# First 256 tokens' output products on f16 halves split by GpSimd, and the weights' own products read from the magnitude tiles

## The chip, the cores and the metric

One core of one Trainium2 chip runs the whole program. The metric is the device time of one launch in microseconds (us); the kernel before takes 868.63 us, the median of three runs.

## The reference

Causal attention with a decay bias, then a feed-forward stage. All inputs come as 64-bit floats, cut here to what is computed:

```python
B, H, S, D = 8, 8, 576, 64                        # q, k, v: [B, H, S, D], s: [B, H, S]
scores = q @ k.transpose(0, 1, 3, 2) / sqrt(D)
cum = cumsum(maximum(s, 0), axis=-1)
bias = -(cum[:, :, :, None] - cum[:, :, None, :])
scores = where(causal, -1e9, scores + minimum(bias, 0))
attn = softmax(scores)
x = (attn @ v).transpose(0, 2, 1, 3).reshape(4608, 512)
h = maximum(maximum(x @ w1, x @ w2), x @ w3)       # w1, w2, w3: [512, 768]
out = h @ w_out                                   # w_out: [768, 512]
```

## The kernel before, in words

**Steps.** The attention is cut into 160 steps. A step is one block of 128 queries (the last of a batch has 64) of one pair of heads. Batches 0 and 1 are visited first with their query blocks 0 and 1, all four pairs of heads, then with their blocks 2, 3, 4; batches 2 to 7 follow whole. In step t the program issues, in this order: work entered with `soon` for this step, a first number of feed-forward groups, the scores of step t+2, work entered with `amid`, the softmax of step t, work entered with `at` (`todo`), a second number of groups, and the products with v. [...]

**Softmax chain.** TensorE (PE) writes the scores `s`, VectorE (DVE) takes their maximum `nm`, ScalarE (ACT) the exponential and its sum `se`, DVE the reciprocal `ri`, ACT the f16 high halves `prh`, DVE the f16 low halves `prl`; DMAs transpose them and PE multiplies with v into `av`. The scores of a later step wait for `prl` of an earlier one, since they reuse its accumulation banks.

**Feed-forward groups.** When all heads of a set of 256 or 320 tokens are done, groups of matmuls for the set are put into `queue`. GROUPS gives for each step how many leave the queue before the scores and how many after. The first set (tokens 0 to 255 of batch 0, `PLAIN`, `add_plain`) is computed in 32-bit floats: 18 groups `up` (4 matmuls of 256 columns each) and 4 groups `down` (6 matmuls each). Every 32-bit matmul leaves two records in the trace. All other sets use f16 high and low halves of both factors: 18 groups `h_group` of 12 matmuls and 4 groups `o_group` of 18. The groups of `up` are maximised in `hs`, two tiles of 128x768 f32; `down` reads them.

**Weights.** The 24 weight tiles arrive as 64-bit words in `r` (`raw_w`) and are decoded by a chain: `decode1` (ACT) makes the 32-bit magnitude tile `t` (`half`, 3 buffers), `shift`, `low_bits` and `sign` (DVE, lines 872, 876, 883) complete it, and `sign` writes the finished f32 weight back over the low words. Later `decode3` (ACT) and `decode4` (DVE, L939) make the f16 halves `w`. A common power of two for the f16 scale comes from `gram1` (L894): the weights' bf16 top halves multiplied with themselves, summed in a corner of the bank `av`; its maximum goes through `wscale1` and `wscale2`. Tiles 0 to 17 (kind "u") give one scale, 18 to 23 ("d") the other. `gram1` reads the raw 64-bit words, so successive values lie 8 bytes apart. It is issued in parts of 5, 4, 4, 2, 3 tiles and of 4, 2: the last part of each kind ahead of the scores (`soon`), the others after them (`at`).

```python
top = raw_w[i].bitcast(BF16).rearrange("p (n t) -> p n t", t=4)[:, :, 1]
for c in range(NKT):
    blk_c = top[:, c * P:(c + 1) * P]
    nc.tensor.matmul(gr, lhsT=blk_c, rhs=blk_c, ...)
```

GpSimd (POOL) has little to do in the first 120 us; from batch 1's first f16 set on it casts and subtracts the f16 halves of the hidden values (L972, L973), and it makes a part of the keys' low halves `qkl` (L494).

Of the kernel before, what the change touches and what calls it, by code (L numbers as in the profile page):

```python
# [21 lines left out]
def kernel(  # L22
# [828 lines left out]


    PLAIN = {(0, 0)}
    W = {}
    fresh = {}
    T = {}
# [7 lines left out]
        return w[:, :, 0], w[:, :, 1]  # L864

    def decode1(i):
        half[i] = moe.tile([P, N], F32, tag="t", name=f"t{i}", bufs=3)
        nc.scalar.activation(out=half[i], in_=words(i)[1], func=AF.Copy, scale=2.0 ** -112)

    def shift(i):  # L870
# [8 lines left out]

    def sign(i):  # L880
        lo, hi = (x.bitcast(I32) for x in words(i))
        ti = half.pop(i).bitcast(I32)
        nc.vector.scalar_tensor_tensor(
            out=lo, in0=hi, scalar=-(2 ** 31), in1=ti, op0=ALU.bitwise_and, op1=ALU.bitwise_or
        )
        new[i] = words(i)[0].rearrange("p (a c) -> p a c", c=P)

    def gram1(kind, n, ids, of):
        gr = bank[:, 3 * P:4 * P]
        for a, i in enumerate(ids):  # L890
# [61 lines left out]
    def add_set(b, ph):  # L952
        q0, nq = PH[ph]
        t0 = b * S + q0
        u = f"{b}_{ph}"
        xs = [(t[:, 0], t[:, 1]) for t in X.pop((b, ph))]
        st = {}

        def h_group(ft, i):
            pm = ps_m.tile([P, 512], F32, tag="m", name=f"pm{u}_{ft}_{i}")  # L960
            w = W[3 * ft + i]
            n = 0
            for kt in range(NKT):
                xh, xl = xs[kt]
                for wt, xt in ((0, xh), (0, xl), (1, xh)):
                    nc.tensor.matmul(  # L966
                        pm[:, :nq], lhsT=w[:, wt, kt, :], rhs=xt, start=(n == 0), stop=(n == 3 * NKT - 1)
                    )
                    n += 1

            def rest(m1):
                nc.gpsimd.tensor_copy(out=st["hh"][:, ft, :nq], in_=m1[:, :nq])  # L972
                nc.gpsimd.tensor_tensor(  # L973
                    out=st["hl"][:, ft, :nq], in0=m1[:, :nq], in1=st["hh"][:, ft, :nq], op=ALU.subtract
                )

            def ev():
                if i == 0:
                    st["m1"] = moe.tile([P, 320], F32, tag="m1", name=f"m1{u}_{ft}", bufs=3)
                    nc.scalar.activation(out=st["m1"][:, :nq], in_=pm[:, :nq], func=AF.Copy, scale=HSC)  # L980
                else:
                    m1 = st["m1"]
                    nc.vector.scalar_tensor_tensor(  # L983
                        out=m1[:, :nq], in0=pm[:, :nq], scalar=HSC, in1=m1[:, :nq], op0=ALU.mult, op1=ALU.max
                    )
                if i == 2:
                    if not st.get("hh"):
                        st["hh"] = moe.tile([P, NFT, 320], F16, tag="hh", name=f"hh{u}")
                        st["hl"] = moe.tile([P, NFT, 320], F16, tag="hlo", name=f"hl{u}")
                    later.append(lambda m1=st["m1"]: rest(m1))  # L990

            pending.append(ev)
            if (ft, i) == (NFT - 1, 2):
                done.add((b, ph))

        def o_group(dt):
            drain()
            flush()
            if dt == 0:
                st["os"] = small.tile([P, 1], F32, tag="os", name=f"os{u}")  # L1000
                nc.gpsimd.tensor_scalar(
                    out=st["os"], in0=OS[b, ph if b < NB else 1], scalar1=WS["kw"], scalar2=None, op0=ALU.mult
                )
            pm = ps_m.tile([P, 512], F32, tag="m", name=f"po{u}_{dt}")
            n = 0
            for ft in range(NFT):
                for wt, ht in ((0, "hh"), (0, "hl"), (1, "hh")):
                    nc.tensor.matmul(  # L1008
                        pm[:, :nq], lhsT=W[18 + ft][:, wt, dt, :], rhs=st[ht][:, ft, :nq],
                        start=(n == 0), stop=(n == 3 * NFT - 1),  # L1010
                    )
# [12 lines left out]
        for dt in range(NDT):
            queue.append((lambda dt=dt: o_group(dt), W, range(18, 24), 18 * nq * NSEC))

    def add_plain(b, ph):
        q0, nq = PH[ph]
        t0 = b * S + q0
        u = f"{b}_{ph}"  # L1030
        xs = X.pop((b, ph))
        hs = {}

        def up(ft, i):
            pm = ps_m.tile([P, 512], F32, tag="m", name=f"pm{u}_{ft}_{i}")
            for kt in range(NKT):
                nc.tensor.matmul(
                    pm[:, :nq], lhsT=T[3 * ft + i][:, kt, :], rhs=xs[kt], start=(kt == 0), stop=(kt == NKT - 1)
                )

            def ev():
                a = ft // 3
                if a not in hs:
                    hs[a] = moe.tile([P, 3, nq], F32, tag=("hh", "hlo")[a], name=f"h{u}_{a}")
                m1 = hs[a][:, ft % 3]
                if i == 0:
                    nc.scalar.activation(out=m1, in_=pm[:, :nq], func=AF.Copy)
                else:
                    nc.vector.tensor_tensor(out=m1, in0=pm[:, :nq], in1=m1, op=ALU.max)

            pending.append(ev)
            if (ft, i) == (NFT - 1, 2):
                done.add((b, ph))

        def down(dt):
            drain()
            pm = ps_m.tile([P, 512], F32, tag="m", name=f"po{u}_{dt}")
            for ft in range(NFT):
                nc.tensor.matmul(
                    pm[:, :nq], lhsT=T[18 + ft][:, dt, :], rhs=hs[ft // 3][:, ft % 3], start=(ft == 0), stop=(ft == NFT - 1)  # L1060
                )

            def ev():
                o_t = moe.tile([P, 320], F32, tag="m1", name=f"o{u}_{dt}", bufs=3)
                nc.scalar.activation(out=o_t[:, :nq], in_=pm[:, :nq], func=AF.Copy)
                nc.sync.dma_start(out=outT[dt * P:(dt + 1) * P, t0:t0 + nq], in_=o_t[:, :nq])

            pending.append(ev)

        for ft in range(NFT):  # L1070
            for i in range(3):
                queue.append((lambda ft=ft, i=i: up(ft, i), T, (3 * ft + i,), 16 * nq * NSEC))
        for dt in range(NDT):
            queue.append((lambda dt=dt: down(dt), T, range(18, 24), 24 * nq * NSEC))

    later = []

# [36 lines left out]
    def soon(t, f, *a):  # L1114
        early.setdefault(t, []).append((f, a))
# [51 lines left out]
    def at(t, f, *a):  # L1167
# [28 lines left out]
    )  # L1196
    GROUPS = (
# [13 lines left out]
    )  # L1211
    scaled = {}
    for kind, tiles, parts in (("u", range(18), (5, 4, 4, 2, 3)), ("d", range(18, 24), (4, 2))):
        ids = sorted(tiles, key=lambda i: begun[i])
        scaled[kind] = end = begun[ids[-1]] + 2
        for n, size in enumerate(parts):
            part = ids[sum(parts[:n]):sum(parts[:n + 1])]
            t = begun[part[-1]] + 2
            (soon if t == end else at)(t, gram1, kind, n, part, len(parts))
        at(end, wscale1, kind)  # L1220
    at(scaled["d"] + 1, wscale2, "d")
    for v in range(NP, len(visits), NP):
# [211 lines left out]
```

## Time and profile before

| | |
|---|---|
| three runs | 867.27, 868.63, 869.16 us |
| span of the profiled execution | 867.7 us; the page gives no other time for it, so its own time is taken as 867.7, 0.9 us under the median |
| PE busy | 815.8 us, 94% |
| DVE busy | 629.2 us, 73% |
| ACT busy | 542.7 us, 63% |
| POOL busy | 287.2 us, 33% |
| chain that ended last | PE 51%, of it the first feed-forward products (L966) 31% |

The table is read from the page of the profiled execution. Shares are averages over a program whose stages differ: an opening in which weights are decoded, a long middle in which attention and feed-forward groups alternate on PE, and a tail of some 88 us without attention. Times inside the program are counted from the start of the span.

### The profile page before, as it was taken

To read this page: it belongs to the slowest core of one execution; us is meant where nothing else is said; L and a number is where in the kernel's file an instruction comes from. 1 tells how busy PE (TensorE), PEld (TensorE's weight loads), DVE (VectorE), ACT (ScalarE), POOL (GpSimd) and SP (SyncE) were. 2 spreads that over 40 slices of the span, in tenths; PEclk is the share of its full clock that TensorE was granted. 3 is DMA by queue.
4 is the path that set the end of the run, shared out by engine and by line. 5 is a ranking of instruction groups with operands and counts; after the bars stand their busy time and mean duration, and the time that the engine had idled before them with its cause. 6 is when DMAs were issued, how large, how long until landed. Compare 5 with 4: busy or idle time off the path is not lost.

```text
span 867.7 us, 19554 instructions
## 1 busy us (share of the span) xinstructions
PE 815.8 (94%) x6929; PEld 617.7 (71%) x6929; DVE 629.2 (73%) x1562; ACT 542.7 (63%) x1458; POOL 287.2 (33%) x532
## 2 busy tenths in 40 slices
PE   5888998989998989899999999999999999999998
PEld 3777777766675667666777677776776678767875
DVE  6979977767778778787887869786878777662110
ACT  5878785576576666656776667666676676653111
POOL 1001115734423324345242524352334425211211
PEclk9999999999999989999999999999999999999999
DMA  9933577866777667765776767767876556433000
GB/s 353 357 89 82 123 160 151 189 151 122 153 153 146 126 156 169 156 120 141 146 167 140 144 135 145 153 129 155 175 154 127 117 111 125 103 75 70 13 14 31
DMA packets 238466, 119.84 MB, mean 138 GB/s; under 512 B 210592, under 2 KB 219296, under 8 KB 238368
## 3 DMA queue, kind: packets, MB, share of 16 engines
q1 hardware_dynamic: 237792, 117.01, 60.4%
q10 hardware_dynamic: 576, 1.57, 0.5%
q8 instruction: 55, 0.90, 0.4%
q14 instruction: 43, 0.35, 0.2%
HBM read 45.12 MB, written 9.44 MB: 63 GB/s over the span
## 4 chain that ended last, share of the span: by engine, by line
PE 51%; DVE 5%; ACT 2%; issue 2%; DMA 1%; SPq 0%; DVEq 0%; ACTq 0%
PE pm L966 31%; PE po L1008 10%; PE av L834 4%; PE s L541 4%; DVE prl L706 2%; PE s L552 1%; ACT prh L703 1%; DVE fixed L161 1%; DVE s L644 1%; DVE m L983 1%; DMA fixed<-in_pair_dram 0%; ACT s L663 0%; DMA pl<-prl 0%; ACT fixed L157 0%; DVE vl L520 0%
## 5 line engine op out<-in xcount | busy, mean ns | idle before, releaser
L966 PE MATMUL pm<-x,w 128*128 128x320 f16 (+1 forms) x3240 | 425.2, 288 | 0.0
L966 PEld LDWEIGHTS <-w 128*128 128x128 f16 x3240 | 312.3, 98 | 90.7 <-issue 4.1
L703 ACT ACTIVATE prh<-s,ri 128x512 f16<-128x512 f32 (+3 forms) x272 | 136.6, 548 | 125.6 <-DVE ri L687 124.4
L706 DVE SCALAR_TENSOR_TENSOR prl<-s,ri,prh 128x512 f16<-128x512 f32 (+3 forms) x272 | 147.0, 577 | 54.6 <-ACT prh L703 31.0
L972 POOL CAST hh<-m 128x320 f16<-128x320 f32 (+1 forms) x90 | 46.2, 513 | 353.8 <-DVE m L983 264.8
L663 ACT ACTIVATE s<-s,nm 128x128 f32<-128x128 f32 (+4 forms) x272 | 145.0, 533 | 17.1 <-DVE nm L644 11.5
L983 DVE SCALAR_TENSOR_TENSOR m<-pm,m 128x320 f32<-128x320 f32 (+1 forms) x180 | 82.1, 456 | 98.1 <-PE pm L966 78.4
L1008 PE MATMUL po<-hh,w 128*128 128x320 f16 (+1 forms) x720 | 142.0, 288 | 0.0
L1008 PEld LDWEIGHTS <-w 128*128 128x128 f16 x1080 | 104.1, 98 | 29.9 <-issue 1.4
L644 DVE CUSTOM_DVE_ANT_0 s<-s,later,qf 128x128 f32<-128x128 f32 (+1 forms) x192 | 106.1, 552 | 14.8 <-PE s L541 11.0
L1008 PE MATMUL po<-hl,w 128*128 128x320 f16 (+1 forms) x360 | 103.6, 288 | 0.0
L186 POOL COPY h<-fixed 64x576 f16<-64x576 f16 x96 | 68.1, 736 | 57.3 <-DVE fixed L161 55.9
L980 ACT ACTIVATE m<-pm 128x320 f32<-128x320 f32 (+1 forms) x90 | 36.6, 407 | 71.9 <-PE pm L966 70.6
L973 POOL TENSOR_TENSOR hl<-m,hh 128x320 f16<-128x320 f32 (+1 forms) x90 | 70.2, 780 | 7.4
L1016 ACT ACTIVATE o<-po,os 128x320 f32<-128x320 f32 (+1 forms) x60 | 30.0, 500 | 55.9 <-PE po L1008 52.1
L834 PEld LDWEIGHTS <-vh 128*64 128x64 f16 x800 | 43.9, 111 | 22.7 <-issue 16.3
L541 PE MATMUL s<-h 128*128 128x128 f16 (+1 forms) x192 | 42.2, 299 | 12.6 <-DVE prl L706 10.8
L663 ACT ACTIVATION_READ_ACCUMULATOR s<-s,nm 128x1 f32 x272 | 53.9, 198 | 0.0
L834 PE MATMUL av<-ph,vh 128*64 128x320 f16 (+3 forms) x368 | 48.8, 286 | 1.7 <-DMA ph<-prh 1.7
L834 PE MATMUL av<-ph,vl 128*64 128x320 f16 (+3 forms) x368 | 44.2, 278 | 0.0
L161 DVE SCALAR_TENSOR_TENSOR fixed<-fixed,qf,fixed 128x576 f16<-128x576 f32 x48 | 42.7, 924 | 1.0 <-ACT fixed L157 0.9
L541 PE MATMUL s<-l 128*128 128x128 f16 (+1 forms) x192 | 41.9, 299 | 0.0
(204 smaller groups left out, 1055.4 us busy)
## 6 DMA issues: line engine op xcount, KB each, us to landing
fixed<-in_pair_dram SPq DMA_DIRECT2D x24, 576.0 KB, 4.5
r<-in_w_dram SPq DMA_DIRECT2D x22, 512.0 KB, 8.3
rv<-in_qkv_dram SPq DMA_DIRECT2D x32, 320.0 KB, 3.5
h<-fixed SPq DMA_DIRECT2D x48, 144.0 KB, 3.4
l<-fixed SPq DMA_DIRECT2D x48, 144.0 KB, 3.6
out_dram<-o SPq DMA_DIRECT2D x32, 160.0 KB, 2.0
out_dram<-o SPq DMA_DIRECT2D x32, 128.0 KB, 1.9
raw<-in_qkv_dram SPq DMA_DIRECT2D x8, 480.0 KB, 3.7
```

Of the source, the lines that this page charges most:

```text
L161: nc.vector.scalar_tensor_tensor(out=u[:, 3 - 3 * x], in0=R[v][("rq", "rk")[x]], scalar=QK[visits[v][0]]["qk"[x]], in1=u[:, 1 + x], op0=AL ...
L186: nc.gpsimd.tensor_copy(out=R[v]["h"][own, j, x], in_=staged(v)[own, 3 - x])
L541: nc.tensor.matmul(ps[:, j, :nk], lhsT=w[:, c, qs], rhs=w[:, 1 - c, 0:nk], start=(x == "h"), stop=(x == "l"), skip_group_check=True,)
L644: nc.vector.tensor_tensor_reduce(out=sc[:, j], in0=sc[:, j], in1=future[0][:, Q4 - nk:Q4], scale=n, scalar=3.0e38, op0=ALU.add, op1=ALU.mi ...
L663: nc.scalar.activation(out=E[t][:, j, :nk] if plain else sc, in_=sc, func=AF.Exp, bias=nm[:, j:j + 1], scale=-1.0 if below(t) else 1.0, ac ...
L703: nc.scalar.activation(out=hi, in_=src, func=AF.Copy, scale=sc)
L706: nc.vector.scalar_tensor_tensor(out=lo, in0=src, scalar=sc, in1=hi, op0=ALU.mult, op1=ALU.subtract)
L834: nc.tensor.matmul(av[j * D:(j + 1) * D, c0:nq], lhsT=lt, rhs=rt, start=(n < 2), stop=(n >= len(todo) - 2), skip_group_check=True,)
L966: nc.tensor.matmul(pm[:, :nq], lhsT=w[:, wt, kt, :], rhs=xt, start=(n == 0), stop=(n == 3 * NKT - 1))
L973: nc.gpsimd.tensor_tensor(out=st["hl"][:, ft, :nq], in0=m1[:, :nq], in1=st["hh"][:, ft, :nq], op=ALU.subtract)
L983: nc.vector.scalar_tensor_tensor(out=m1[:, :nq], in0=pm[:, :nq], scalar=HSC, in1=m1[:, :nq], op0=ALU.mult, op1=ALU.max)
L1008: nc.tensor.matmul(pm[:, :nq], lhsT=W[18 + ft][:, wt, dt, :], rhs=st[ht][:, ft, :nq], start=(n == 0), stop=(n == 3 * NFT - 1),)
```

## The change

1. `gram1` takes one tile, reads the top halves of the magnitude tile `t` (values 4 bytes apart), and all tiles are issued with `soon`, two steps after their `decode1`, ahead of the scores. The tiles `t` get 5 buffers, and a buffer is free when PE has read it, no longer when `sign` has.
2. The 4 `down` groups of the first set become 18 f16 matmuls of 256 columns each, with the f16 halves of tiles 18 to 23. GpSimd makes the f16 halves of `hs`: a factor `hf`, then for each of two tiles a scaling in place, a cast and a subtraction. These are issued at the start of step 18. The `down` groups no longer follow the `up` groups in the queue; they are put in after the fourth `h_group` of the next set.
3. GROUPS[18] goes from (1, 1) to (2, 2).
4. `dynamic_dma_scratch_size=1024` is given to the program's constructor.

```diff
     def decode1(i):
-        half[i] = moe.tile([P, N], F32, tag="t", name=f"t{i}", bufs=3)
+        half[i] = moe.tile([P, N], F32, tag="t", name=f"t{i}", bufs=5)
...
     def sign(i):
-        ti = half.pop(i).bitcast(I32)
+        ti = half[i].bitcast(I32)
...
-    def gram1(kind, n, ids, of):
+    def gram1(kind, i, begin, end):
         gr = bank[:, 3 * P:4 * P]
-        for a, i in enumerate(ids):
-            top = raw_w[i].bitcast(BF16).rearrange("p (n t) -> p n t", t=4)[:, :, 1]
-            for c in range(NKT):
...
+        top = half.pop(i).bitcast(BF16).rearrange("p (n t) -> p n t", t=2)[:, :, 1]
+        for c in range(NKT):
...
         for ft in range(NFT):
             for i in range(3):
                 queue.append((lambda ft=ft, i=i: h_group(ft, i), W, (3 * ft + i,), 12 * nq * NSEC))
+                if (ft, i) == (1, 0):
+                    queue.extend(downs)
+                    downs.clear()
...
+        def halves():
+            f = small.tile([P, 2], F32, tag="hf", name=f"hf{u}", bufs=1)
+            ts = nc.gpsimd.tensor_scalar
+            ts(out=f[:, 0:1], in0=WS["u"], scalar1=VS[b, 1], scalar2=HSC, op0=ALU.mult, op1=ALU.mult)
+            ts(out=f[:, 1:2], in0=OS[b, 1], scalar1=WS["kw"], scalar2=None, op0=ALU.mult)
+            st["os"] = f[:, 1:2]
+            st["hh"] = moe.tile([P, NFT, nq], F16, tag="hp", name=f"hh{u}")
+            st["hl"] = moe.tile([P, NFT, nq], F16, tag="hq", name=f"hl{u}")
+            for a in range(2):
+                h, r = hs[a], slice(3 * a, 3 * a + 3)
+                ts(out=h, in0=h, scalar1=f[:, 0:1], scalar2=None, op0=ALU.mult)
+                nc.gpsimd.tensor_copy(out=st["hh"][:, r], in_=h)
+                nc.gpsimd.tensor_tensor(out=st["hl"][:, r], in0=h, in1=st["hh"][:, r], op=ALU.subtract)
+
         def down(dt):
...
             for ft in range(NFT):
-                nc.tensor.matmul(
-                    pm[:, :nq], lhsT=T[18 + ft][:, dt, :], rhs=hs[ft // 3][:, ft % 3], start=(ft == 0), stop=(ft == NFT - 1)
-                )
+                for wt, ht in ((0, "hh"), (0, "hl"), (1, "hh")):
+                    nc.tensor.matmul(
+                        pm[:, :nq], lhsT=W[18 + ft][:, wt, dt, :], rhs=st[ht][:, ft], start=(n == 0), stop=(n == 3 * NFT - 1)
+                    )
+                    n += 1
...
-        for dt in range(NDT):
-            queue.append((lambda dt=dt: down(dt), T, range(18, 24), 24 * nq * NSEC))
+        soon(HALVES, halves)
+        downs.extend((lambda dt=dt: down(dt), W, range(18, 24), 18 * nq * NSEC) for dt in range(NDT))
...
-            t = begun[part[-1]] + 2
-            (soon if t == end else at)(t, gram1, kind, n, part, len(parts))
+        for i in ids:
+            soon(max(begun[i] + 2, 0), gram1, kind, i, i == ids[0], i == ids[-1])
...
     GROUPS = (
-        0), (1, 0), (2, 1), (1, 1), (1, 0), (1, 1), (1, 1), (0, 0), (1, 0), (1, 0), (3, 0), (2, 1), (1, 2),
+        0), (1, 0), (2, 1), (1, 1), (1, 0), (1, 1), (2, 2), (0, 0), (1, 0), (1, 0), (3, 0), (2, 1), (1, 2),
```

What this does to the order of instructions, in three places. The first is PE in step 0, where the parts of `gram1` begin (`pp` is the product that spreads the reciprocals in the first steps, `s_230` and `s_242` are the same scores of step 2, `t_154`, `t_194`, `t_214` three magnitude tiles):

```order
 L737 MATMUL pp_227<-dg_223,e_209 128x128 x2
-L564 MATMUL s_230<-st_89,q_192 128x128 x2
-L570 MATMUL s_230<-kb_177,qr_180 128x128 x2
+L895 LDWEIGHTS t_154
+L895 MATMUL av<-t_154 128x128
...
+L895 MATMUL av<-t_194 128x128
...
+L895 MATMUL av<-t_214 128x128
...
+L564 MATMUL s_242<-st_89,q_192 128x128 x2
+L570 MATMUL s_242<-kb_177,qr_180 128x128 x2
```

Three tiles, 12 matmuls, now stand ahead of these scores; before, they were part of the 20 that followed the scores of step 4.

The second is GpSimd, between two of its key subtractions (L494): what is new there, steps 18 on.

```order
 L494 TENSOR_TENSOR qkl_1247<-raw_981,qkh_1124 128x576
 L504 TENSOR_SCALAR q_1250<-blk,qr_180 128x128
...
+L1061 TENSOR_SCALAR hf_0_1363<-swu,inv_1_1308 128x1
+L1062 TENSOR_SCALAR hf_0_1363<-p_1_1306,kw 128x1
+L1068 TENSOR_SCALAR h_0_0_745<-h_0_0_745,hf_0_1363 128x768
+L1069 CAST hh_0_1366<-h_0_0_745 128x768
+L1070 TENSOR_TENSOR hl_0_1367<-h_0_0_745,hh_0_1366 128x768
+L1068 TENSOR_SCALAR h_0_1_1042<-h_0_1_1042,hf_0_1363 128x768
+L1069 CAST hh_0_1366<-h_0_1_1042 128x768
+L1070 TENSOR_TENSOR hl_0_1367<-h_0_1_1042,hh_0_1366 128x768
+L972 CAST hh_0_1444<-m_0_0_1391 128x256
```

Two chains of scaling, cast and subtraction over 128x768 stand where GpSimd had nothing, and the first split of the next set (L972) has come ahead of the next key subtraction.

The third is PE in step 18. Before, with the queue down to the `down` groups:

```order
L595 MATMUL s_1287<-kb_177,qr_180 128x384 x2
...
L1059 MATMUL po_0_0_1337<-h_0_1_1042,r_494 128x256
L595 MATMUL s_1344<-qkh_1124 128x512 x2
...
L1059 MATMUL po_0_1_1374<-h_0_0_745,r_598 128x256
...
L615 MATMUL s_1397<-qkh_1124 128x256
```

and with the change:

```order
L966 MATMUL pm_0_0_0_1337<-x_0_902,w_721 128x256
...
L966 MATMUL pm_0_0_1_1350<-x_0_902,w_721 128x256
...
L595 MATMUL s_1374<-qkh_1124 128x512 x2
...
L966 MATMUL pm_0_0_2_1404<-x_0_902,w_724 128x256
...
L966 MATMUL pm_0_1_0_1417<-x_0_902,w_724 128x256
...
L615 MATMUL s_1450<-qkh_1124 128x256
```

Around the scores of 512 columns, one `down` group on either side has given way to two f16 groups of the next set on either side; the four `down` groups come in the following steps. From there on the queue is two groups ahead of where it was, until it runs empty, ahead of batch 2's first set, and the two programs agree from there to the end.

## Rows read from the trace of the kernel before

**Rows 1.** Busy time by stretch: stretch, length, PE, PEld, DVE, ACT, POOL, granted clock, DMA share, GB/s.

```profile
24.00:54.00 30.00, 24.39 (x202) 21.09 (x202) 27.89 (x66) 22.98 (x73) 0.00 (x0) 0.99 0.72 266
105.89:115.87 9.98, 9.67 (x52) 7.53 (x53) 9.80 (x21) 6.61 (x14) 0.00 (x0) 1.00 0.39 75
115.87:130.99 15.12, 14.64 (x118) 12.07 (x118) 9.61 (x17) 13.18 (x34) 3.49 (x5) 1.00 0.99 211
```

**Rows 2.** Timeline of DVE, its waits in the opening: start, duration, instruction, count [wait <- releaser].

```profile
18.27 0.42 DVE L649 TENSOR_REDUCE nm<-s 128x2 f32<-128x256 f32 x1 [0.83 <-PE s L575]
...
33.18 0.43 DVE L872 TENSOR_SCALAR t<-t 128x512 int32<-128x512 int32 x1 [0.36 <-ACT t L868]
...
39.20 0.69 DVE L649 TENSOR_REDUCE nm<-s 128x2 f32<-128x512 f32 x1 [0.27 <-PE s L575]
...
51.39 0.29 DVE L901 TENSOR_REDUCE amwu<-av 128x1 f32<-128x128 f32 x1 [1.24 <-PE av L894]
```

**Rows 3.** Timeline of PE at 17 and 24 us: the same scores twice, and the first part of `gram1`.

```profile
17.00 0.80 PE L564 MATMUL s<-st,q 64*128 64x128 f32 x4
...
24.25 0.49 PE L564 MATMUL s<-st,q 64*128 64x128 f32 x4
...
24.86 2.52 PE L894 MATMUL av<-r 128*128 128x128 bf16 x20
```

**Rows 4.** Timeline of PE at 317 us: 128x128 f16 products on contiguous operands, and what follows.

```profile
316.88 0.28 PE L541 MATMUL s<-l 128*128 128x128 f16 x2
316.99 0.71 PE L966 MATMUL pm<-x,w 128*128 128x256 f16 x5
```

**Rows 5.** Timeline of PE: a 32-bit `down` group, and three f16 groups of 256 columns.

```profile
113.21 2.81 PE L1059 MATMUL po<-h,r 128*128 128x256 f32 x12
...
127.14 4.09 PE L966 MATMUL pm<-x,w 128*128 128x256 f16 x36
```

**Rows 6.** Groups of POOL by shape: instruction, count, busy us, mean ns, idle before.

```profile
L231 POOL TENSOR_TENSOR bias<-bias,pieces 64x576 f32<-64x576 f32 x2 | 2.5, 1273 | 0.2
L229 POOL CAST pieces<-bias 64x576 f16<-64x576 f32 x3 | 2.0, 659 | 0.2
L227 POOL TENSOR_SCALAR bias<-bias,bscale 64x576 f32<-64x576 f32 x1 | 1.7, 1747 | 0.1
```

**Rows 7.** Timeline of DVE, from 106 to 132 us.

```profile
106.82 0.16 DVE L471 RECIPROCAL inv<-p 128x1 f32<-128x1 f32 x1
...
111.19 1.41 DVE L939 SCALAR_TENSOR_TENSOR w<-r,swd,w 128x512 f16<-128x512 f32 x2
...
115.64 0.88 DVE L520 SCALAR_TENSOR_TENSOR vl<-rv,inv,vh 128x640 f16<-128x640 f32 x1
118.60 0.56 DVE L497 SCALAR_TENSOR_TENSOR qkl<-raw,qkh 128x384 fp32r<-128x384 f32 x1 [2.08 <-ACT qkh L484]
...
131.05 0.96 DVE L983 SCALAR_TENSOR_TENSOR m<-pm,m 128x256 f32<-128x256 f32 x2 [0.85 <-ACT m L980]
```

**Rows 8.** Timelines of POOL and DVE at 198 us, then at 81 us.

```profile
198.38 0.80 POOL L973 TENSOR_TENSOR hl<-m,hh 128x320 f16<-128x320 f32 x1
...
198.42 1.44 DVE L520 SCALAR_TENSOR_TENSOR vl<-rv,inv,vh 128x640 f16<-128x640 f32 x1
...
81.11 0.63 POOL L504 TENSOR_SCALAR q<-blk,qr 128x128 fp32r<-128x128 bf16 x1
...
81.23 0.52 DVE L520 SCALAR_TENSOR_TENSOR vl<-rv,inv,vh 128x256 f16<-128x256 f32 x1
```

**Rows 9.** Timeline of PE before batch 2's first set: the scores that begin an interval.

```profile
289.78 0.34 PE L541 MATMUL s<-h 128*128 128x128 f16 x2 [0.62 <-DVE prl L706]
...
296.14 0.38 PE L541 MATMUL s<-h 128*128 128x256 f16 x2 [0.20 <-DVE prl L706]
...
301.47 0.49 PE L541 MATMUL s<-h 128*128 128x384 f16 x2
...
310.11 0.42 PE L552 MATMUL s<-h 128*64 128x256 f16 x2 [2.76 <-DVE prl L706]
```

More of the change, by code (lines that the diff above doesn't have):

```diff
@@ L853 @@
     PLAIN = {(0, 0)}
+    HALVES = 18
+    downs = []
     W = {}
@@ L886, in sign @@
         new[i] = words(i)[0].rearrange("p (a c) -> p a c", c=P)
-    def gram1(kind, n, ids, of):
+    def gram1(kind, i, begin, end):
         gr = bank[:, 3 * P:4 * P]
-        for a, i in enumerate(ids):
-            top = raw_w[i].bitcast(BF16).rearrange("p (n t) -> p n t", t=4)[:, :, 1]
-            for c in range(NKT):
-                blk_c = top[:, c * P:(c + 1) * P]
-                nc.tensor.matmul(
-                    gr, lhsT=blk_c, rhs=blk_c, start=(n == 0 and a == 0 and c == 0),
-                    stop=(of == n + 1 and a == len(ids) - 1 and c == NKT - 1), skip_group_check=True,
-                )
+        top = half.pop(i).bitcast(BF16).rearrange("p (n t) -> p n t", t=2)[:, :, 1]
+        for c in range(NKT):
+            blk_c = top[:, c * P:(c + 1) * P]
+            nc.tensor.matmul(
+                gr, lhsT=blk_c, rhs=blk_c, start=(begin and c == 0), stop=(end and c == NKT - 1), skip_group_check=True,
+            )
     def wscale1(kind):
@@ L1031, in add_plain @@
         xs = X.pop((b, ph))
-        hs = {}
+        hs, st = {}, {}
         def up(ft, i):
@@ L1057, in down @@
             pm = ps_m.tile([P, 512], F32, tag="m", name=f"po{u}_{dt}")
+            n = 0
             for ft in range(NFT):
-                nc.tensor.matmul(
-                    pm[:, :nq], lhsT=T[18 + ft][:, dt, :], rhs=hs[ft // 3][:, ft % 3], start=(ft == 0), stop=(ft == NFT - 1)
-                )
+                for wt, ht in ((0, "hh"), (0, "hl"), (1, "hh")):
+                    nc.tensor.matmul(
+                        pm[:, :nq], lhsT=W[18 + ft][:, wt, dt, :], rhs=st[ht][:, ft], start=(n == 0), stop=(n == 3 * NFT - 1)
+                    )
+                    n += 1
             def ev():
                 o_t = moe.tile([P, 320], F32, tag="m1", name=f"o{u}_{dt}", bufs=3)
-                nc.scalar.activation(out=o_t[:, :nq], in_=pm[:, :nq], func=AF.Copy)
+                nc.scalar.activation(out=o_t[:, :nq], in_=pm[:, :nq], func=AF.Copy, scale=st["os"])
                 nc.sync.dma_start(out=outT[dt * P:(dt + 1) * P, t0:t0 + nq], in_=o_t[:, :nq])
@@ L1212 @@
     scaled = {}
-    for kind, tiles, parts in (("u", range(18), (5, 4, 4, 2, 3)), ("d", range(18, 24), (4, 2))):
+    for kind, tiles in (("u", range(18)), ("d", range(18, 24))):
         ids = sorted(tiles, key=lambda i: begun[i])
         scaled[kind] = end = begun[ids[-1]] + 2
-        for n, size in enumerate(parts):
-            part = ids[sum(parts[:n]):sum(parts[:n + 1])]
-            t = begun[part[-1]] + 2
-            (soon if t == end else at)(t, gram1, kind, n, part, len(parts))
+        for i in ids:
+            soon(max(begun[i] + 2, 0), gram1, kind, i, i == ids[0], i == ids[-1])
         at(end, wscale1, kind)
@@ L1389 @@
     from concourse.bass_utils import run_bass_kernel_spmd as _run
-    nc = _bacc.Bacc("TRN2", target_bir_lowering=False, num_devices=1)
+    nc = _bacc.Bacc("TRN2", target_bir_lowering=False, num_devices=1, dynamic_dma_scratch_size=1024)
     arrays, args = {}, []
```

## The prediction

> **What bounds the kernel now.** The page's shares (PE 94%, DVE 73%) say that PE is the bound of the whole. I read the busy time by stretch next, because both parts of this change lie in the first 131 us [rows 1]. The reader is to compare DVE and PE in each line. From 24 to 54 us DVE works 27.89 of 30.00 us and PE 24.39: the opening, where weights are decoded, is DVE's. From 105.89 to 115.87 both are nearly full, DVE with 9.80 of 9.98 us and PE with 9.67. From 115.87 to 130.99 it is PE's, 14.64 of 15.12 us against 9.61 of DVE. So a microsecond taken from PE in the opening counts only where DVE waits for PE.
>
> The third view is DVE's timeline with its waits [rows 2]. Four matter: 0.83 us at 18.27 and 0.27 at 39.20 for scores, 0.36 at 33.18 for a decoded tile, and 1.24 at 51.39 for the end of `gram1`. A matmul put ahead of scores lengthens a wait of the first kind; a faster last part of `gram1` shortens the last.
>
> **Gram, the price.** The trace shows 20 of its matmuls in 2.52 us, 0.126 us each [rows 3]. Two 128x128 f16 products start at 316.88 and the next work at 316.99, 0.055 us each [rows 4]. That is a contiguous operand; the new operand has values 4 bytes apart, between that and the 8 bytes of now. The page shows no such operand, so the bounds are 0.055 and 0.126. I take 0.055, since half of each 4 bytes is used and the row of the slow case skips twice as far. In steps before about 22 us everything on PE is slower: the same four records of scores take 0.80 us at 17.00 and 0.49 at 24.25 [rows 3], a factor of 1.63.
>
> [...]
>
> **Gram, the sum.** Of 96 matmuls, those of tiles "u" now all stand ahead of scores.
> - Step 0 issues 12 ahead of the scores that begin at 17.00: 12 x 0.055 x 1.63 = 1.08 us, all added to the wait at 18.27, as PE had waited before it and has nothing in hand. +1.1.
> - At 33.18 DVE waited 0.36 us for ACT, which waits for a weight's DMA and is not moved: DVE comes later and finds the tile there. -0.4.
> - Ahead of the scores for 39.20 stand 8 matmuls, 8 x 0.055 = 0.44 us. DVE waited there already, so they count. +0.4.
> - Between these, the parts of 20 and 16 matmuls leave their places behind the scores: 0, since DVE doesn't wait for PE there. The cover is DVE's 93%.
> - The last 12 matmuls before 51.39 shrink by 12 x 0.071 = 0.85 us of the wait of 1.24. -0.8.
>
> Together +0.3. Bounds: if the 12 and 8 matmuls are hidden by something that I don't see, -1.2; if all keep 0.126 us, 2.4 + 0.6 - 0.4 = +2.6. The 24 matmuls of tiles "d" (steps 9 to 14) lie where neither the scores nor DVE waited for them: 0. `decode1` now waits until PE has read a tile, with five buffers in place of three: 0, since `gram1` runs two steps behind `decode1`, no later than `sign` did.
>
> **Down groups.** A 32-bit group takes 2.81 us; 36 f16 matmuls take 4.09, so 18 take 2.05 [rows 5]. Four groups save 4 x 0.76 = 3.0 us of PE. But GROUPS[18] pulls two groups of 12 forward, 24 x 0.114 = 2.7 us. In steps 18 to 22 PE so does 0.3 us less, step 18 has almost the same load as before (four groups of 1.36 in place of two of 2.81), steps 20 and 21 lose 0.8 each, and step 22 gains 1.4. What DVE and ACT allow decides, so I count 0 for it. The saving proper comes out only where the queue runs empty, two groups earlier (below).
>
> **GpSimd's halves.** Prices per element from [rows 6]: 64x576 took 1.75 us to scale, 0.66 to cast, 1.27 to subtract; 768 elements are 1.33 times as many: 2.33, 0.88, 1.70, so 4.9 us per tile and 9.8 for both. `hf` waits for `inv`, ready at 106.98 [rows 7]. That gives scaling 107.0 to 109.3, cast to 110.2, subtraction to 111.9, scaling to 114.2, cast to 115.1, subtraction to 116.8. GpSimd was busy for 0.00 us until 115.87 [rows 1], and the `down` groups come 3 us and more later: its own time costs 0. Queued behind it are the first split of the next set and a key subtraction, 2.6 us of work by the same prices; GpSimd was busy for only 3.49 of the 15.12 us from 115.87 on [rows 1], so they fit: 0.
>
> What costs is DVE beside it. A GpSimd subtraction from 198.38 to 199.18 stretched a DVE instruction with two operands in SBUF from 0.88 us [rows 7] to 1.44 [rows 8]: it lost the remainder, 0.76, less 0.2. A GpSimd scaling at 81.11 did nothing of the kind: the DVE instruction begun in it took 0.52 us and ended with it [rows 8]. So casts and subtractions hold DVE, scalings don't. In the plan above the two `w` at 111.19 meet the first subtraction and lose 0.7 - 0.2 = 0.5 us, in the stretch that is DVE's. The `vl` at 115.64 meets the second and loses about 1.0, but DVE waits 2.08 us next, at 118.60 [rows 7]: hidden. +0.5; bounds 0 and, if both and a cast count, +2.3.
>
> [...]
>
> **Two groups brought forward** also bring their evacuations: two DVE instructions of 0.48 us, as the pair at 131.05 [rows 7]. One falls ahead of 115.87, where DVE is full, one behind: +0.5 (bounds 0 and +1.0). The `down` groups that they displace had theirs on ACT.
>
> **Where the queue runs empty.** Until then the program is two groups ahead. The interval from 289.78 held one group of 24 matmuls and one of 18, now three of 18: 12 more of 320 columns, 12 x 0.142 (0.114 x 320/256) = +1.7. The next, from 296.14 to 301.47, held two of 18, now one. It can fall from 5.33 only as far as the softmax chain lets it: the two intervals from 301.47 to 310.11 take 8.64 us and end with PE waiting 2.76 for `prl` [rows 9], so 4.3 each, -1.0. The two last gain 0, as that wait takes what PE saves. Together +0.7; bounds -2.7 (PE's work alone) and +1.7. From there on both programs are the same.
>
> **Sum**: +0.3 +0 +0.5 +0.5 +0.7 = +2.0 us on the profiled execution of 867.7, which is 0.9 under the median of 868.63. On the median: 870.6. About 0.2%, 1.7 us, is what a measurement of this kernel can tell from no change.
>
> **Rivals.**
> - **C, faster:** PE stays the bound everywhere. The place is 105.89 to 130.99 and the empty queue at 296. PE's 3.0 us come back in full, and the last part of `gram1` gives 0.85 with the opening's additions hidden: 868.6 - 3.85 = 864.8. For it: PE is 97% busy in both stretches [rows 1]. Against: the two groups are cashed only where PE waits for the chain already. It decides if the 2.76 us wait at 310.11 moves forward by as much as PE is ahead.
> - **D, no change:** DVE isn't held (its operands come at other times than GpSimd's) and the evacuations fit its gaps; of opening and queue end +1.0 remains, and 0.5 comes back in steps 20 and 21, where PE is the bound and does 0.8 less in each: 869.1. For it: the plan of GpSimd is no surer than a microsecond, and the hold hangs on 0.7 of one. Against: DVE has no gap of 0.48 before 115.87.
> - **B:** GpSimd holds DVE for scalings too. The `w` right behind `inv` at 106.98 meet the first, those after 111.19 the second, and each loses the remainder, at most 2.33 - 0.2 = 2.1 us; DVE is so full that it asks early, so I take three quarters, 1.6 each: 870.6 + 3.2 = 873.8. It decides if the first `w` after `inv` takes over 1 us.
> - **E:** the 4-byte operand is no faster than the 8-byte one. The opening then costs +2.6 in place of +0.3: 872.9.
>
> **How the numbers follow.** My forecast 0.33, C 0.27, D 0.23, B 0.08, E 0.09. Faster by over 0.2% is C, 0.27. Within 0.2% (866.9 to 870.4): D and a third of my own case, which its bounds spread from about 869 to 873: 0.33. Slower: the rest, 0.40. The range goes from C's 864.8 to 874.0, past E and B.
>
> **What would show it.** `gram1` at 0.055 to 0.07 us a matmul, and the wait at 18.27 near 1.9 us, the one at 51.39 near 0.4; the scores of step 2 about 1 us late and everything to 50 us with them. At 107 to 117 us six long GpSimd instructions, a `w` on DVE above 1.0 us in place of 0.7, and no held instruction beside a scaling. At the end of the queue a first interval near 8 us and a second near 4.3. I am wrong if the scores that now begin at 115.87 come earlier than that, if the scores of 310.11 come more than 1 us earlier than those of 115.87 do, or if `gram1` keeps 0.12 us.

## The result, and the profile after

The changed kernel takes 882.16 us (median of 4 runs, 879.67 to 883.94); the kernel before took 868.89 us beside it. The ratio is 1.0145, 95% interval 1.0118 to 1.0171: slower by 1.45%, some 13 us, and outside my range. The profiled execution took 880.41 us with a span of 878.6. Its first lines of the page:

```profile
PE 809.0 (92%) x6953; PEld 611.6 (70%) x6953; DVE 632.6 (72%) x1562; ACT 542.0 (62%) x1458; POOL 298.4 (34%) x540
```

PE is busy for 6.8 us less than before, and the span is 10.9 longer. So the time went into waits. To find them I took from both PE timelines the start of each of the 160 scores and subtracted. The table gives after minus before, worked out in that way: how late the changed kernel is at the scores of a step, and what the stretch up to there added.

| scores of step | before | after | late by | added since the line above |
|---|---|---|---|---|
| 10 | 51.20 | 51.03 | -0.17 | |
| 20 | 111.96 | 110.50 | -1.46 | -1.29 |
| 21 | 115.87 | 118.01 | +2.14 | +3.60 |
| 24 | 130.99 | 132.69 | +1.70 | -0.44 |
| 28 | 157.11 | 160.97 | +3.86 | +2.16 |
| 30 | 165.57 | 172.99 | +7.42 | +3.56 |
| 42 | 230.03 | 236.46 | +6.43 | -0.99 |
| 43 | 235.76 | 244.43 | +8.67 | +2.24 |
| 48 | 261.57 | 270.24 | +8.67 | 0.00 |
| 55 | 289.78 | 301.40 | +11.62 | +2.95 |
| 59 | 310.11 | 322.24 | +12.13 | +0.51 |

Behind step 59 the two programs are the same, and nothing more is lost (1.3 us come back by the last scores). The opening is as good as unchanged; there is one loss at step 20, where GpSimd's halves run, and there are several far behind it, where nothing of the change is issued.

**Step 20.** The timeline of DVE in the changed kernel (columns as in [rows 7]):

```profile
110.94 0.42 DVE L983 SCALAR_TENSOR_TENSOR m<-pm,m 128x256 f32<-128x256 f32 x1 [0.57 <-ACT m L980]
111.29 2.79 DVE L939 SCALAR_TENSOR_TENSOR w<-r,swd,w 128x512 f16<-128x512 f32 x2
114.00 1.52 DVE L520 SCALAR_TENSOR_TENSOR vl<-rv,inv,vh 128x640 f16<-128x640 f32 x1
...
116.72 1.14 DVE L706 SCALAR_TENSOR_TENSOR prl<-s,ri,prh 128x384 f16<-128x384 f32 x2
```

The timeline of POOL beside it:

```profile
106.17 1.28 POOL L1061 TENSOR_SCALAR hf<-swu,inv 128x1 f32<-128x1 f32 x1 [7.05 <-DVE inv L471]
107.55 0.69 POOL L1062 TENSOR_SCALAR hf<-p,kw 128x1 f32<-128x1 f32 x1
108.20 2.22 POOL L1068 TENSOR_SCALAR h<-h,hf 128x768 f32<-128x768 f32 x1
110.49 0.82 POOL L1069 CAST hh<-h 128x768 f16<-128x768 f32 x1
111.40 2.13 POOL L1070 TENSOR_TENSOR hl<-h,hh 128x768 f16<-128x768 f32 x1
113.51 2.65 POOL L1068 TENSOR_SCALAR h<-h,hf 128x768 f32<-128x768 f32 x1
116.23 0.82 POOL L1069 CAST hh<-h 128x768 f16<-128x768 f32 x1
117.14 1.65 POOL L1070 TENSOR_TENSOR hl<-h,hh 128x768 f16<-128x768 f32 x1
```

And the scores of step 21 in PE's timeline:

```profile
118.01 0.35 PE L615 MATMUL s<-qkh 128*128 128x256 f32 x1 [3.46 <-DVE prl L706]
```

The two `w` took 1.41 us before [rows 7] and 2.79 beside the first subtraction; `vl` took 0.88 and now 1.52, beside the second scaling, which itself took 2.65 in place of 2.22. That is 2.02 us of DVE. The wait of 0.57 and an evacuation of 0.42, 0.99 together, are the first of the groups brought forward. The two sums make the 3.04 by which steps 19 and 20 together are longer (-0.56 and +3.60 by the same subtraction). `prl` ends late, and PE waits 3.46 us for it where it had not waited.

**Step 28**, the clearest of the later ones. The timeline of DVE before, around the last evacuations of a step with three groups:

```profile
154.59 0.42 DVE L983 SCALAR_TENSOR_TENSOR m<-pm,m 128x256 f32<-128x256 f32 x1 [0.45 <-PE pm L966]
155.90 0.42 DVE L983 SCALAR_TENSOR_TENSOR m<-pm,m 128x256 f32<-128x256 f32 x1 [0.89 <-PE pm L966]
156.25 0.88 DVE L520 SCALAR_TENSOR_TENSOR vl<-rv,inv,vh 128x640 f16<-128x640 f32 x1
...
159.39 0.75 DVE L706 SCALAR_TENSOR_TENSOR prl<-s,ri,prh 128x512 f16<-128x512 f32 x1
```

The same instructions in the changed kernel:

```profile
159.84 0.43 DVE L983 SCALAR_TENSOR_TENSOR m<-pm,m 128x256 f32<-128x256 f32 x1 [2.19 <-PE pm L966]
161.07 0.42 DVE L983 SCALAR_TENSOR_TENSOR m<-pm,m 128x256 f32<-128x256 f32 x1 [0.81 <-PE pm L966]
161.42 0.87 DVE L520 SCALAR_TENSOR_TENSOR vl<-rv,inv,vh 128x640 f16<-128x640 f32 x1
...
164.56 0.75 DVE L706 SCALAR_TENSOR_TENSOR prl<-s,ri,prh 128x512 f16<-128x512 f32 x1
```

The reader is to look at what DVE does next after the second `m`: `vl`, then the softmax up to `prl`, for which PE's next scores wait. The three groups start at 153.07 before and at 156.58 after. Before, the second `m` came 2.83 us after that, when PE had done two groups; now it comes after 4.49, when PE has done all three (the 36 matmuls took 4.46 us here and 4.10 before, so 0.4 of the delay is PE's; its clock is looked at below). Of three successive groups the first is evacuated by ACT (`i == 0`), the two others by DVE. With a queue that is two ahead, the two for DVE are the second and third of this step; they were the first and second. PE's next scores then waited 2.19 us for `prl` in place of 0.88, by PE's timeline before and after:

```profile
160.48 0.49 PE L595 MATMUL s<-qkh 64*128 64x512 f32 x2 [0.88 <-DVE prl L706]
...
165.65 0.50 PE L595 MATMUL s<-qkh 64*128 64x512 f32 x2 [2.19 <-DVE prl L706]
```

**Step 29** had three groups of 12; now the third is the set's first output group, 18 matmuls, directly behind the group that completes its operand. Timeline of PE after:

```profile
166.90 2.78 PE L966 MATMUL pm<-x,w 128*128 128x256 f16 x24
...
172.11 0.27 PE L1008 MATMUL po<-hh,w 128*128 128x256 f16 x1 [0.79 <-POOL hh L972]
172.86 0.27 PE L1008 MATMUL po<-hl,w 128*128 128x256 f16 x1 [0.48 <-POOL hl L973]
```

It waits 1.27 us for GpSimd's split of the last values, a wait that the trace of before hasn't got, and is 6 x 0.114 = 0.7 us longer. In step 42 two groups of 18 stand where two of 12 stood. What one step gets, another gives up, but not in time: steps 44 and 45 have 12 matmuls in place of 18, and their lengths change by -0.18 and +0.18 us.

**The clock.** Some of the later lateness isn't the program's. The granted clock of PE was 0.50 for 6.80 us ahead of the scores of step 28, twice as long as the 3.40 before, and once more, for 3.30 us, in step 52; from 157.30 to 160.00 us, just behind the first of these, it was 0.99. Busy time by stretch after (columns as in [rows 1]):

```profile
150.50:157.30 6.80, 6.23 (x42) 4.87 (x43) 4.69 (x10) 3.04 (x9) 3.27 (x4) 0.50 0.61 186
287.10:290.40 3.30, 3.30 (x22) 1.86 (x22) 3.27 (x8) 1.58 (x5) 2.24 (x3) 0.50 0.34 69
```

and before:

```profile
149.00:152.40 3.40, 3.40 (x24) 2.53 (x25) 2.73 (x6) 1.27 (x2) 3.01 (x4) 0.50 0.54 127
```

Two kernels below, e8 and e4, run the same groups there (e8 up to step 38), with a granted clock of 0.50 only as long as before ahead of the scores of step 28, and e4 not at all in step 52. From step 24 to 28 they lose 0.2 and 0.6 us in place of the 2.2 of the table; from 48 to 55 e4 loses 1.9 in place of 2.95. So 2.6 to 3.0 us of the table go with the clock. The whole times point the same way: the granted clock averages 0.983 over the four runs of the changed kernel and 0.990 over the 87 recorded runs of the kernel before, and among those 87 each 0.001 less goes with 0.52 us more (a straight line through them). By that estimate 3.6 of the 13 us go with the clock. Whether the longer waits of PE bring it down is not shown; e2 below has the same lead at 0.988 and is no faster.

### The profile page after: what moved, and what is told of

Read it like the earlier page. It is cut to its first block, busy times and chain, and to the rows that moved or that the text cites. A ratio compares the mean times of both kernels' runs of the same rounds, so it can differ in the third digit from the quotient of the medians.

```text
span 878.6 us, 19598 instructions
## 1 busy us (share of the span) xinstructions
PE 809.0 (92%) x6953; PEld 611.6 (70%) x6953; DVE 632.6 (72%) x1562; ACT 542.0 (62%) x1458; POOL 298.4 (34%) x540
## 4 chain that ended last, share of the span: by engine, by line
PE 61%; DVE 9%; ACT 6%; DMA 4%; issue 4%; POOL 1%; SPq 1%; ACTq 0%; DVEq 0%; POOLq 0%
PE pm L966 36%; PE po L1008 12%; PE av L834 6%; PE s L541 4%; DVE prl L706 3%; DMA pl<-prl 2%; ACT prh L703 2%; ACT s L663 2%; PE s L552 1%; DMA rv<-in_qkv_dram 1%; DVE m L983 1%; DVE fixed L161 1%; DVE s L644 1%; ACT fixed L157 1%; DMA out_dram<-o 1%
## 5 line engine op out<-in xcount | busy, mean ns | idle before, releaser
L972 POOL CAST hh<-m 128x320 f16<-128x320 f32 (+1 forms) x90 | 45.4, 504 | 355.8 <-DVE m L983 283.6
```

## The experiments

**Whose loss is it?** Four kernels. Theory Q, formed after the result: the queue's lead of two groups, kept from step 24 to 59, costs most. Theory H: the lateness behind GpSimd's halves is carried on and grows. Rival G: the new order of `gram1` sets off the later waits.

e1, gram alone: parts 1 and 4 on the kernel before. Part 4 goes with it, to make room for five tiles `t`.

> Only part 1 of the change: gram1 from the magnitude tiles (with part 4, which makes room for five of them); first set's output products in 32 bits and GROUPS as before. In the changed kernel the scores of step 20 come 1.46 us earlier than before, so theory Q (the loss is the queue running two groups ahead) and theory H (the loss starts with GpSimd's halves holding VectorE) both expect 1 to 1.5 us faster, 867 to 868. A rival G, by which the new order of the gram products sets off the later waits, expects over 875.

869.29 us, ratio 0.9999 (0.9982 to 1.0016). The gram part neither gains nor loses within 1.5 us either way; the 1 us that Q and H expected isn't there, and neither is G's loss.

e2, the lead alone:

```diff
-        0), (1, 0), (2, 1), (1, 1), (1, 0), (1, 1), (1, 1), (0, 0), ...
+        0), (1, 0), (2, 1), (1, 1), (1, 0), (1, 1), (2, 2), (0, 0), ...
```

> The kernel before with GROUPS[18] (2, 2) and nothing else: no halves on GpSimd, old gram1. Theory Q expects most of the loss here: the changed kernel lost about 9 us between the scores of steps 21 and 59, so 876 to 879. Theory H expects no more than what my sum had for the empty queue and the moved groups, 868 to 870.

883.28 us, ratio 1.0151 (1.0115 to 1.0187): with one entry of the table and nothing else, as slow as the whole change, and above the 876 to 879 that Q expected. 4.5 us of it are lost by step 24, as four 32-bit groups stand in step 18; from step 24 to 59 it loses 8.4. Its single losses are those of the changed kernel: 1.32 and 2.27 in steps 28 and 29 (there 1.31 and 2.25), 2.24 in step 42 (2.24).

e3, the change without the lead (GROUPS[18] back at (1, 1)):

> The changed kernel with GROUPS[18] back at (1, 1): halves, f16 down groups and gram1 as in the change, but the queue no longer two ahead. Theory Q expects 869 to 872: the local loss of about 3 us behind the halves, less the gram's gain of 1 and the 3 us saved on the down groups as far as they count. Theory H expects the loss to stay, 878 to 882.

873.81 us, ratio 1.0059 (1.0039 to 1.0078). The steps from the scores of 28 to those of 59 are as before to 0.2 us each, but for one that is 1.0 shorter; so Q holds. At step 20 it still loses 3.5 us: without the lead's evacuation ahead of them the two `w` meet a cast and the subtraction and take 3.35 us, `vl` 1.52, which is 2.6 us of DVE. It is above 872, by something that neither theory had: now three `down` groups fall into one step, and ACT, which evacuates them, waits for a buffer. Timeline of ACT in e3:

```profile
134.28 0.47 ACT L1085 ACTIVATE o<-po,hf 128x256 f32<-128x256 f32 x1 [1.49 <-PE po L1078]
...
143.23 0.47 ACT L1085 ACTIVATE o<-po,hf 128x256 f32<-128x256 f32 x1 [6.76 <-DMA out_dram<-o]
```

e4, the change with the old `gram1`:

> The changed kernel with gram1 as before (raw words, five and two parts): halves, f16 down groups, queue two ahead. Theories Q and H both expect the changed kernel's time plus the gram's gain of 1 to 1.5 us, 883 to 884. Rival G expects that the loss is gone, 868 to 871.

882.62 us, ratio 1.0147 (1.0111 to 1.0184), as the change itself and just under the expected 883 to 884. G falls.

**Where does the lead cost, and what of step 20?** Four kernels again. e5 gives the lead back by step 23; e6 does so too and splits the halves; e7 does so too and moves them; e8 gives the lead back at step 38 and not before.

```diff
-        ..., (2, 2), (0, 0), (1, 0), (1, 0), (3, 0), (2, 1), (1, 2),
+        ..., (2, 2), (0, 0), (1, 0), (1, 0), (2, 0), (1, 1), (1, 2),
```

> The changed kernel with GROUPS[22] (2, 0) and GROUPS[23] (1, 1): the halves, the f16 down groups and step 18 as in the change, but the two groups' lead is given back by step 23, so that from step 24 on every step has the groups it had before. Theory Q (running two groups ahead from step 24 to 59 costs some 8 to 10 us) expects 868 to 873: what remains is the hold behind the halves, 3.6 us at step 20, of which steps 21 to 23 give back 1 to 3. Theory H (the lateness of step 20 itself is carried on and grows) expects 879 to 883.

871.48 us, ratio 1.0019 (0.9999 to 1.0039). Two entries of the table take away 1.26% of the loss of 1.45%. From step 24 to 59 e5 loses 1.3 us where the change loses 10.4 (2.6 to 3.0 of them with the clock). H falls: both have the same loss at step 20 (3.5 and 3.6 us).

e6:

```diff
-            for a in range(2):
-                h, r = hs[a], slice(3 * a, 3 * a + 3)
+            for ft in range(NFT):
+                h = hs[ft // 3][:, ft % 3]
```

> As e5, with the halves in six pieces of 128x256 in place of two of 128x768. If a VectorE instruction is held for the remainder of one GpSimd instruction, pieces of a third hold it for a third, and the 3.6 us at step 20 shrink to 1 to 2: 1 to 2.5 us below e5. If VectorE loses by GpSimd's total busy time beside it, the same as e5 or a little more.

871.43 us, ratio 1.0020 (0.9998 to 1.0042). The loss at step 20 shrinks from 3.5 to 2.2 us, as expected of instructions a third as long, but the total doesn't tell it apart from e5, where 1 to 2.5 us less were expected.

e7, with e5's two entries and a scratch of 512 bytes in place of 1024 (both left out here):

```diff
-    HALVES = 18
+    HALVES = 20
...
-        soon(HALVES, halves)
+        at(HALVES, halves)
...
-                if (ft, i) == (1, 0):
+                if (ft, i) == (2, 1):
...
-                    hs[a] = moe.tile([P, 3, nq], F32, tag=("hh", "hlo")[a], name=f"h{u}_{a}")
+                    hs[a] = moe.tile([P, 3, nq], F32, tag=("h0", "h1")[a], bufs=1, name=f"h{u}_{a}")
```

> As e5, with the halves moved from the start of step 18 to the end of step 20, behind the key subtraction there, where VectorE works 9.61 of 15.12 us, and the down groups four places later in the queue (the 32-bit hidden values get buffers of their own for that). If the loss at step 20 is VectorE held by the halves in its full stretch, the scores of step 21 come within 1 us of where they came before, relative to those of step 20, and the total is 865 to 868, below both kernels. If the loss comes from the two groups in front of the scores of step 20 and 21, it stays: 869 to 872.

871.05 us, ratio 1.0004 (0.9985 to 1.0023). At step 20 the loss falls to 1.5 us, not under 1: the halves' hold of 2.0 is gone, the 0.99 of the groups brought forward stays, and the rest is that the scores of step 20 begin 0.55 earlier than before. Timeline of DVE in e7, the same instructions as in step 20 above:

```profile
112.95 0.43 DVE L983 SCALAR_TENSOR_TENSOR m<-pm,m 128x256 f32<-128x256 f32 x1 [0.57 <-ACT m L980]
113.29 1.41 DVE L939 SCALAR_TENSOR_TENSOR w<-r,swd,w 128x512 f16<-128x512 f32 x2
114.61 0.88 DVE L520 SCALAR_TENSOR_TENSOR vl<-rv,inv,vh 128x640 f16<-128x640 f32 x1
```

`w` and `vl` have their old durations back, the `m` with its wait stays. The total misses 865 to 868; steps 24 to 26 lose 5.8 us. The timeline of ACT in e7:

```profile
149.41 0.47 ACT L1085 ACTIVATE o<-po,hf 128x256 f32<-128x256 f32 x1 [6.49 <-DMA out_dram<-o]
...
154.68 0.47 ACT L1085 ACTIVATE o<-po,hf 128x256 f32<-128x256 f32 x1 [2.16 <-DMA out_dram<-o]
```

The same wait in the changed kernel's timeline of ACT:

```profile
130.65 0.47 ACT L1085 ACTIVATE o<-po,hf 128x256 f32<-128x256 f32 x1 [0.72 <-DMA out_dram<-o]
...
135.58 0.47 ACT L1085 ACTIVATE o<-po,hf 128x256 f32<-128x256 f32 x1 [2.75 <-DMA out_dram<-o]
```

The outputs of the `down` groups share three buffers (`m1`) with the maxima of the next set's groups. Before, the first set's output groups were through before those began to use them.

e8, GROUPS[38] (1, 1) in the changed kernel:

> The changed kernel with GROUPS[38] (1, 1) in place of (2, 2): the lead is given back at step 38 in place of the empty queue at step 55. Theory Q expects the losses behind step 42 to go (2.2 us at step 42, some 3 from 48 to 54, 0.5 at 55 to 59): 876 to 877. Theory H expects 881 to 883.

874.35 us, ratio 1.0052 (1.0029 to 1.0076), 2 us better than expected. Steps 28 and 29 lose 1.31 and 2.26 as in the change, step 42 loses nothing (2.24 there) and steps 43 to 59 lose 0.1 (3.5 there). Each of these losses stands and falls with the groups of its own step. Up to step 38 this is the changed kernel's program, and ACT waits 0.30, 2.94 and 1.74 us for output buffers in it; yet it loses 0.2 us from step 24 to 28.

**Is it the pattern of evacuations?** Two more kernels: e9 has the halves in six pieces as e6, GROUPS as before, and spreads the `down` groups; e10 makes the lead three, with GROUPS[24] (2, 2) in place of (1, 2). The new lines of e9:

```diff
-                if (ft, i) == (1, 0):
-                    queue.extend(downs)
-                    downs.clear()
+                if downs and 3 * ft + i > 2:
+                    queue.append(downs.pop(0))
```

> Towards a version that keeps the saving: GROUPS as in the kernel before, halves in six pieces at step 18, and the four f16 down groups put in one by one behind the fourth to seventh h_group, so that no step has three of them and no lead is built up. Theory Q, with the hold of the pieces (2.2 - 1.5 = 0.7 us) and PE's 3.0 us saved in steps 18 to 24, expects 866 to 869 (-0.3% to 0). If what counts in steps 20 to 27 is the evacuation of the down groups (their output DMA holds the buffers), it stays at 871 to 873, as e5 and e6.

870.80 us, ratio 1.0019 (1.0001 to 1.0038): above 869, with ACT still waiting 2.87 us for an output's buffer.

> The changed kernel with GROUPS[24] (2, 2) in place of (1, 2): the queue runs three groups ahead from step 25 on, in place of two. Each third group is evacuated by ScalarE, the two others by VectorE, so with a lead of three every step has its old pattern of evacuations, with a lead of two it hasn't. If the 1.31 us of step 28 come from VectorE waiting for the last group of the step before it can go on with the softmax, as the trace of the changed kernel shows, they are gone with three (0 to 0.3 us). If they come from the lead as such (PE later or earlier with its load), they stay at 1.3 or grow. Step 29, where output groups replace first products, grows in both cases. Whole: 880 to 884.

881.37 us, ratio 1.0145 (1.0117 to 1.0174). Timeline of DVE in e10 at step 28, whose three groups start at 156.00:

```profile
157.72 0.42 DVE L983 SCALAR_TENSOR_TENSOR m<-pm,m 128x256 f32<-128x256 f32 x1
158.83 0.42 DVE L983 SCALAR_TENSOR_TENSOR m<-pm,m 128x256 f32<-128x256 f32 x1 [0.69 <-PE pm L966]
159.17 0.88 DVE L520 SCALAR_TENSOR_TENSOR vl<-rv,inv,vh 128x640 f16<-128x640 f32 x1
...
161.27 0.75 DVE L282 TENSOR_REDUCE qm<-fixed 128x1 f32<-128x576 f32 x1 [0.63 <-DMA fixed<-in_pair_dram]
```

The second `m` comes 2.83 us after the start, exactly as before the change: the old pattern is back. Step 28 still loses 0.79 us, not 0 to 0.3: 0.63 is a new wait for a load. Steps 48 to 54, which lose 2.95 in the change and 1.9 in e4 with a lead of two, lose 0.2 with three, at the same PE load per step but for the last. So there the loss is the pattern, not the lead. Step 29 grows from 2.25 to 3.24, with two output groups in place of one, and step 41 from 0.67 to 2.59. From step 24 to 59 the sum is 9.2 us.

**A version that keeps the saving.** e11 is e7 (with its scratch of 512), e12 is e6, each with the first set's outputs in the buffers of the magnitude tiles, which are idle by then:

```diff
-                o_t = moe.tile([P, 320], F32, tag="m1", name=f"o{u}_{dt}", bufs=3)
+                o_t = moe.tile([P, N], F32, tag="t", name=f"o{u}_{dt}", bufs=5)
```

> As e7 (halves late, lead given back), with the first set's four output tiles in the buffers of the magnitude tiles, which are free by then, in place of the three buffers that they share with the groups' maxima. In e7 ScalarE waited 6.49 and 2.16 us for the output DMAs to release such a buffer, and with it the softmax: steps 24 to 26 lost 5.8 us. If the buffers are the cause, these waits go and steps 24 to 26 lose under 1.5 us: 864 to 867, 0.4 to 0.7% below before. If the cause is the load on TensorE in these steps, it stays at 870 to 872.

867.28 us, ratio 0.9978 (0.9958 to 0.9998), the median just above the expected 864 to 867, the ratio 0.2% below before where 0.4 to 0.7% were expected. ACT's waits for the output DMA are gone, and what steps 24 to 26 lose falls from 5.8 us to 0.3; so these waits were that loss. The 0.2% are barely clear of noise; the kernel is 1.7% below the change.

> As e6 (halves in pieces at step 18, lead given back), with the same buffers for the output tiles. ScalarE waited 3.20 us there, and steps 22 to 26 lost 3.4 us, of which 2.3 came back in steps 26 and 27. Expected 1 to 2 us below e6, 0 to 0.2% below before; the same as e6 if the wait is hidden.

870.32 us, ratio 1.0013 (0.9995 to 1.0030): above what was expected, and not told apart from e6 or from before.

## Why the prediction was wrong

**The step that failed** is the first sentence of "Where the queue runs empty": "Until then the program is two groups ahead." I gave the lead a price at its start and its end and none on the way, 35 steps long, and named no work that would hide it. e5 against the change shows what stood there: 9.1 us from step 24 to 59 (10.4 less 1.3), 2.6 to 3.0 of them with the clock. From step 28 to 59 the lead costs 7.4 us in e2, at a mean granted clock of 0.988 (0.986 in the change), and 7.2 in e4, and it costs nothing in e5, which has given it back. It is evacuations that DVE now makes for PE's last groups (steps 28, 48 to 54) and output groups in place of shorter ones (29, 42). Q is not among my rivals; the range ended at 874.0 without it.

**The hold behind GpSimd** was the right mechanism with the wrong size: 0.5 forecast, 2.0 measured (the change's loss at step 20 less e7's), and 2.6 of DVE in e3, without the lead. Two parts of it failed. The first scaling started 2.1 us behind `inv` in place of at once, as the two tiny instructions for `hf`, which I had at nothing, took from 106.17 to 108.20; so the first subtraction began at 111.40, beside the first `w`, and held the pair for 1.38 us. And the sentence "casts and subtractions hold DVE, scalings don't" fell: `vl` at 114.00 lost 0.64 beside a scaling. For casts [rows 8] has no row; in e9 `vl` took 1.01 us in place of 0.88 when it began 0.59 us behind the start of a cast of 0.93. Rival B had a scaling hold DVE for its remainder, which would have been over 2 us, but `vl` ended 0.64 before the scaling did. Late in a scaling `vl` lost nothing; timelines of POOL and DVE in e10:

```profile
112.81 2.65 POOL L1068 TENSOR_SCALAR h<-h,hf 128x768 f32<-128x768 f32 x1
...
114.62 0.87 DVE L520 SCALAR_TENSOR_TENSOR vl<-rv,inv,vh 128x640 f16<-128x640 f32 x1
```

So a scaling held DVE in a part of its time, and neither B nor my reading of the one row [rows 8] is right; which part and why stays open.

**Evacuations**: 0.5 forecast ahead of the scores of step 21, 0.99 measured (in e7 steps 19 and 20 together). I had priced DVE's 0.48, not the 0.57 that DVE waits for ACT's evacuation ahead of it.

**The output buffers** are a wait that I didn't have at all. I costed the moved `down` groups by PE's time alone; their evacuations go through three buffers that the next set's groups also use, and the release is an output DMA. e11 against e7 is worth 5.5 us in steps 24 to 26 of the two traces, but 0.26% of the time (0.9978 against 1.0004), which is within the noise of the two ratios; e12 isn't told apart from e6.

**Right** was the price of the new operand, which I took at its lower bound, 0.055. Parts of 8 and of 12 products take 0.55 and 0.78 us from their start to the next scores, so four more cost 0.23, 0.057 each; single starts in the trace are 0.057 us apart as well. PE's timeline after:

```profile
24.80 0.62 PE L895 MATMUL av<-t 128*128 128x128 bf16 x8
25.35 0.49 PE L564 MATMUL s<-st,q 64*128 64x128 f32 x4
...
34.38 0.85 PE L895 MATMUL av<-t 128*128 128x128 bf16 x12
35.16 0.49 PE L564 MATMUL s<-st,q 64*128 64x128 f32 x4
```

Contiguous values took 0.055 us [rows 4]; the products of the 8-byte operand start 0.118 us apart in the trace before (0.126 in [rows 3] is the busy time of a part by its count). DVE's two waits came near what was forecast, 2.12 (1.9 forecast) and 0.69 (0.4 forecast), by its timeline after:

```profile
20.12 0.42 DVE L649 TENSOR_REDUCE nm<-s 128x2 f32<-128x256 f32 x1 [2.12 <-PE s L575]
...
51.22 0.29 DVE L901 TENSOR_REDUCE amwu<-av 128x1 f32<-128x128 f32 x1 [0.69 <-PE av L895]
```

By the scores of step 10 the change stands at -0.2 us against +0.3 in my sum. That the sum is right is not shown by it: the ten other kernels with this opening stand there anywhere from -0.4 to +2.2. One bound of the sum was added up wrongly: with 0.126 us for all, the 8 products cost 1.0 and not 0.6, so rival E is some 0.4 us higher than I wrote.

The end of the queue was right too, with +0.7 forecast for steps 55 to 59 and +0.51 measured; the first interval takes 7.82 us (near 8 forecast), the second 4.86 (4.3). In part that is luck: the second gained 0.5 where 1.0 was forecast, and the third gained 0.5 where I had 0. Timeline of PE after, against [rows 9]:

```profile
301.40 0.34 PE L541 MATMUL s<-h 128*128 128x128 f16 x2 [0.86 <-DVE prl L706]
...
309.22 0.38 PE L541 MATMUL s<-h 128*128 128x256 f16 x2
...
314.08 0.50 PE L541 MATMUL s<-h 128*128 128x384 f16 x2 [1.82 <-DVE prl L706]
...
322.24 0.43 PE L552 MATMUL s<-h 128*64 128x256 f16 x2 [2.76 <-DVE prl L706]
```

What stays open: whether the lead lowers the clock, or the runs of the changed kernel met it by chance. Nor was it tried to fit the whole table of groups to the lead of two.

## What to carry to other kernels

An entry in a table that says how many pieces of work a step takes moves every piece behind it, until the queue runs empty. Count what lands in each step on the way: which engine evacuates it, how long it is, whether its operand is just being made; and give the lead back at once if nothing gains from it. Groups that are moved next to others use the same buffers, so look who else takes them and what sets them free.

## What was not expected of the hardware

A GpSimd scaling of 128x768 f32 in place held a DVE instruction with two operands in SBUF for a part of its time only: `vl` took 1.52 us in place of 0.88 when it began 0.49 us behind the scaling (the change), and 0.87 when it began 1.81 us behind it (e10).

Matmuls of 128x128 bf16 whose values lie 4 bytes apart started every 0.057 us, against 0.118 at 8 bytes (the traces after and before) and 0.055 for contiguous f16 ones [rows 4].

In e3 PE had nothing to do for 4.67 us ahead of the scores of step 21; from 119.1 to 122.3 us its granted clock was then 0.50, and the first of these matmuls took 0.55 us in place of 0.36 (before); the three behind it started 0.21 to 0.22 us apart in place of 0.12.
